# Phi prepared a batch earlier, fixed buffers, and a cast on VectorE in the exponential slots

## The chip, the cores and the metric

The kernel runs on one core of a Trainium2 chip. The metric is the device time of one execution in microseconds (us). The core's engines are TensorE (PE in the profile; PEld is its weight load, which overlaps), VectorE (DVE), ScalarE (ACT), GpSimd (POOL, almost unused here) and SyncE (SP, which issues most DMAs). Each works through its own queue in order and waits on semaphores for the others.

## What is computed

An attention through 32 memory slots per head, followed by a feed-forward network of 2048 hidden units with a SiLU. There are 8 batches, 8 heads, 576 rows and 64 elements per head, all in float32.

```python
a = softmax(phi, over the 576 rows)             # phi: 8 x 8 x 576 x 32
k_m = einsum('bhsm,bhsd->bhmd', a, k)
v_m = einsum('bhsm,bhsd->bhmd', a, v)
scores = softmax(q @ k_m.T / 8)                 # over the 32 memory slots
attn_out = scores @ v_m
x = attn_out reshaped to (4608, 512)
h = x @ w_in
return (h * sigmoid(h)) @ w_out
```

## The kernel before

Float32 accuracy is reached with pairs: a high part, rounded to the matmul's fp32r type, and a low part, the difference. Every product is then three matmuls (high by high, high by low, low by high).

The kernel never forms the attention output. For a batch `b` it multiplies `v_m` into `w_in` (`p_mm`, a *projection*, line 621, in four blocks of 512 hidden units). That gives a weight of 256 memory rows, `pm`, and the first layer is attention weights by `pm`. The attention weights, split in high and low, are in `aparts`.

Batches 2 to 7, on which the change works, are alike. A batch is 16 **slots**: two halves `t` of the rows, eight pairs `j` of hidden blocks. A slot, called here batch:slot (5:4 is slot 4 of batch 5), is:

- `ffn1s` (L807): 12 matmuls 128x288 into the PSUM tile `h`, of which there is one;
- `forms` (L813 on): ScalarE applies Silu to `h` (L818 for the 512 main columns, into the one buffer `gbuf`; L820 for the 64 left-over ones), casts the first three of seven forms to their high part (L822); VectorE makes the other four forms (L823, L826, L827); ScalarE casts these (L828); VectorE subtracts for the two low parts (L829, L830);
- the slot's **events**: steps of preparing the next batch, and of projecting this one;
- `st_step` (L839) of the slot *before*: 21 products into four PSUM banks by a Strassen-like scheme. After slots 7 and 15 `st_out` (L870, L875) empties the banks: two copies on ScalarE, seven adds on VectorE.

TensorE's order is the order of the code, ScalarE's too from batch 1 on. VectorE's is put by the framework's scheduler, which must keep events' VectorE work behind the slot's last subtraction (`behind`, `last_split`) except for `s_all`. SP's order is that of the code in the first stage and the scheduler's behind it.

The events prepare batch `n = b + 1` while batch `b` runs. They are: `phi_max` (L256 to L259) and `phi_fold` (three steps, L284 to L302), the maximum over all rows; `phi_sub` (L310, L313) subtracts it; `phi_exp` (L317) is the exponential on ScalarE, which needs another activation table than Silu, so that a table load stands before it and one before the next Silu; `e_mm` (L333, L343) sums phi by keys and values, in two parts of two chunks each; `e_tr` transposes; `s_all` (L380 to L389) makes the scores; `s_max`, `s_sub`, `s_exp` (L432, again between two table loads), `s_sum`, `s_norm` are the second softmax; `s_back` (L453, L458) turns it back and `s_low` (L463) makes the low part, for the rows of the first half (FIRST) or of the second (SECOND). The projection copies its bank pair `bg` out in `p_split`: the high part on ScalarE (L644), the low part on VectorE (L646). `bg` exists once; `e_mm`, `e_tr` and `s_all` use it too.

In batches 2 to 6 the events stood in these slots: 1 `phi_max` and third projection, 2 `phi_fold`, 3 `phi_sub`, then the fourth projection, 4 `phi_exp`, 5 and 7 `e_mm`, 6 `s_back`'s second half (SECOND), 8 `e_tr`, 9 `s_all`, 10 `s_max` and `s_sub`, 11 `s_exp`, 12 `s_sum`, 13 `s_norm` and first projection, 14 `s_back` and `s_low` (FIRST), 15 second projection. Batch 7 prepares nothing and only projects.

After an odd batch the 64 left-over rows of two batches are worked off (`left_split`, L680 and L682, and `left_st`, the `lsum` tiles of L839).

phi, scores and attention weights shared a pool of two buffers (`att`), and the two halves of q one of two (`q`).

Of the kernel before, what the change touches and what calls it, by code (L numbers as in the profile page):

```python
# [48 lines left out]
def attn_ffn_kernel(  # L49
# [155 lines left out]
    at = [dict() for _ in range(B)]  # L205
# [163 lines left out]

    def s_all(b):  # L370

        sc = at[b]["sc"] = sb.tile([P, 2, S], F32, tag="att", name=f"sc{b}")
        bg, left = bgtile(), beside_h(S - 512)
        kvT = at[b]["kvT"]
        w = 512 - HALF
        for hf, f, n in ((0, 0, HALF), (1, 0, w), (1, w, HALF - w)):
# [9 lines left out]
        for p in range(2):
            nc.vector.transpose(sc[:, p, 512:], left[p])
        for p in range(2):
            nc.vector.transpose(sc[:, p, :512], bg[:, p])  # L389

    def s_mm(b, hf):
        if "sc" not in at[b]:
            at[b]["sc"] = sb.tile([P, 2, S], F32, tag="att", name=f"sc{b}")
        pt = banks(b)
        kvT, q = at[b]["kvT"], at[b]["q", hf]
        for r in range(NR):
            for p in range(2):
# [6 lines left out]
        at[b]["sp", hf] = pt
        if b:
            s_turn(b, hf)
# [39 lines left out]
            at[b][x] = aparts[:, k, b == 1].rearrange("p (g s) -> p g s", g=2)  # L446

    def s_back(b, u):
        at[b]["aT"] = sb.tile([P, 2, S], F32, tag="att", name=f"aT{b}")
        set_parts(b)  # L450
        aT, sc = at[b]["aT"], at[b]["sc"]
        for p in range(2):
            nc.vector.transpose(aT[:, p], sc[:, p])  # L453
        s_high(b, u)
# [13 lines left out]
    first = {}  # L468
    UW = (2 * HM, 2 * HM + P)
# [328 lines left out]
    def ffn1s(b, t, j):  # L798
# [11 lines left out]
                    n += 1  # L810
        return h

    def forms(b, t, j, h):  # L813


        g = form_src
        w = MAIN // 2
        nc.scalar.activation(gbuf[:, :MAIN].rearrange("p (i f) -> p i f", i=2), h[:, :, :w], AF.Silu)  # L818
        o = b % 2 * LEFT + t * (LEFT // 2)
        nc.scalar.activation(gleft[:, 2 * j : 2 * j + 2, o : o + LEFT // 2], h[:, :, w:HALF], AF.Silu)  # L820
        hi, lo = form_high[j % 2], form_low[j % 2]
        nc.scalar.activation(hi[:, :3], g[:, 1:4], AF.Copy)  # L822
# [4 lines left out]
        s4 = nc.vector.tensor_tensor(g[:, 7], g[:, 3], g[:, 6], op=ALU.subtract)  # L827
        nc.scalar.activation(hi[:, 3:], g[:, 4:], AF.Copy)  # L828
# [93 lines left out]
    def ev(b, slot, fn, *a):  # L922
        events.setdefault((b, slot), []).append((fn, a))

    for b in range(B):
        n = b + 1
        if b == 0:
            for j in range(2, DFF // CW):
                ev(b, 2 * j - 1.5, p_mm, b, j * CW, CW)
        elif b == 1:  # L930
            ev(b, 0, win_save)
            for j in range(1, NJ):
                ev(b, 4 * j - 3, p_mm, b, j * JW, JW)
# [25 lines left out]
        ev(b, 3 if b > 1 else sub + 0.5, phi_sub, n)  # L959
        ev(b, ex, phi_exp, n)  # L960
        if n < 3:
            ev(b, em, e_mm, n)
            ev(b, 14 if b == 0 else em + 1, load_kv, n + 1, range(FULLC if b == 0 else 2))
        else:
            ev(b, em, e_mm, n, range(2))
            ev(b, em, load_kv, n, range(2, FULLC))
            ev(b, em + 2, e_mm, n, range(2, FULLC))
            if n + 1 < B:
                ev(b, em + 2, load_kv, n + 1, range(2))
# [7 lines left out]
        if n + 1 < B:  # L977
            ev(b, s1, load_q, n + 1, 0)
# [5 lines left out]
        u = ALL if n < 3 else FIRST  # L984
        ev(b, sk, s_back, n, u)
        ev(b, sk, s_low, n, u)
        if n + 1 < B:
            ev(b, sk, load_phi, n + 1)
# [247 lines left out]
```

## Time and profile before

| | us |
|---|---|
| median of 3 runs | 718.83 (717.64 to 719.99) |
| the profiled execution | 719.41 |
| its span, first to last instruction | 717.6 |

The page's section 2 cuts the span in 40 slices; each digit is an engine's busy share in tenths, PEclk the granted clock:

```profile
PE   8999999999998999989999899989999989999997
DVE  4898799789756568947768567884776848786653
ACT  3878674535335455454625545554452454654440
PEclk9999999999999999999999999999999999999999
```

TensorE is busy nearly everywhere; VectorE and ScalarE have room in the mean. A group such as "PE h L807" is read as engine, written tile and line; "<-ACT phi L317" behind a wait says that ScalarE's instruction of line 317 ended it. Since slots are all alike, a longer slot in the same trace shows what an event costs.

### The profile page before, as it was taken

The page shows a single profiled execution, that of the slowest core. Times are in us where ns is not written, and L with a number is a line of the kernel's source. Part 1 is how long each engine was busy: PE and PEld are TensorE (multiplying, and loading weights), DVE is VectorE, ACT ScalarE, POOL GpSimd, SP SyncE. Part 2 cuts the span into 40 slices and gives each one's busy share as a digit, 9 for nine tenths or more (in the row PEclk, how much of TensorE's full clock was granted, in tenths as well). Part 3 has the DMA queues.
Part 4 walks back from the last instruction along what each step waited for, and adds up shares of the span by engine and source line. Part 5 has one row for each costly group of instructions (what it writes and reads, how often), then busy time and mean ns, then how long its engine had stood idle before and what let it go on. Part 6 is the DMA issues. An engine that isn't in the chain of part 4 may idle for free.

```text
span 717.6 us, 14742 instructions
## 1 busy us (share of the span) xinstructions
PE 684.0 (95%) x5932; PEld 601.9 (84%) x5932; DVE 516.8 (72%) x1109; ACT 367.1 (51%) x674; POOL 0.7 (0%) x6
## 2 busy tenths in 40 slices
PE   8999999999998999989999899989999989999997
PEld 3577777888888889879898888879989889889997
DVE  4898799789756568947768567884776848786653
ACT  3878674535335455454625545554452454654440
POOL 0000000000000000000000000000000000000000
PEclk9999999999999999999999999999999999999999
DMA  9997956304531344025330154303631013210001
GB/s 345 330 357 251 338 215 225 104 30 156 195 102 61 110 178 152 31 73 214 120 122 16 60 192 155 122 1 134 213 111 71 16 61 129 91 76 2 30 1 45
DMA packets 32948, 93.90 MB, mean 131 GB/s; under 512 B 2928, under 2 KB 13296, under 8 KB 29296
## 3 DMA queue, kind: packets, MB, share of 16 engines
q1 hardware_dynamic: 31936, 90.19, 36.1%
q10 hardware_dynamic: 944, 2.77, 1.0%
q8 instruction: 47, 0.77, 0.4%
q14 instruction: 21, 0.17, 0.1%
HBM read 77.22 MB, written 15.73 MB: 130 GB/s over the span
## 4 chain that ended last, share of the span: by engine, by line
PE 52%; DVE 20%; ACT 10%; issue 4%; DVEq 0%; ACTq 0%
PE sum L839 18%; PE h L807 12%; PE acc L706 7%; PE lsum L839 5%; PE h L665 4%; ACT aparts L828 3%; DVE gbuf L823 2%; PE bg L628 2%; DVE pm L646 2%; DVE oo L875 2%; DVE gbuf L826 2%; DVE gbuf L827 2%; PE bg L333 2%; ACT gbuf L818 2%; DVE gparts L830 2%
## 5 line engine op out<-in xcount | busy, mean ns | idle before, releaser
L807 PE MATMUL h<-aparts,pm 128*128 128x288 f32 x1152 | 169.0, 296 | 6.4 <-ACT gleft L820 6.4
L807 PEld LDWEIGHTS h<-aparts,pm 128*128 128x128 f32 x1152 | 157.0, 188 | 7.6 <-ACT gleft L820 7.4
L818 ACT ACTIVATE gbuf<-h 128x512 f32<-128x512 f32 x96 | 57.4, 598 | 129.4 <-PE h L807 129.2
L823 DVE TENSOR_TENSOR gbuf<-gbuf 128x256 f32<-128x256 f32 x96 | 40.5, 422 | 114.4 <-ACT gbuf L818 113.9
L828 ACT ACTIVATE aparts<-gbuf 128x512 fp32r<-128x512 f32 x96 | 60.7, 633 | 100.2 <-DVE gbuf L827 100.2
L839 PE MATMUL sum<-wo_hi,aparts 128*128 128x256 f32 x384 | 106.5, 298 | 0.0
L839 PE MATMUL sum<-kept,aparts 128*128 128x256 f32 x576 | 102.4, 287 | 2.2 <-DVE oo L875 2.2
L839 PE MATMUL sum<-wo_lo,aparts 128*128 128x256 f32 x384 | 101.9, 287 | 0.0
L839 PEld LDWEIGHTS sum<-wo_hi,aparts 128*128 128x128 f32 x384 | 74.7, 195 | 21.4 <-ACT gleft L820 14.2
L839 PEld LDWEIGHTS sum<-kept,aparts 128*128 128x128 f32 x576 | 84.3, 195 | 3.4 <-DVE oo L875 3.4
L706 PE MATMUL acc<-wo_hi,gparts 128*128 128x512 f32 x256 | 86.4, 397 | 0.3 <-DVE gparts L682 0.2
L830 DVE TENSOR_TENSOR gparts<-gbuf,aparts 128x512 fp32r<-128x512 f32 x96 | 66.5, 693 | 20.5 <-ACT aparts L828 20.5
L839 PEld LDWEIGHTS sum<-wo_lo,aparts 128*128 128x128 f32 x384 | 75.0, 195 | 0.0
L839 PE MATMUL sum<-wo_hi,gparts 128*128 128x256 f32 x384 | 72.8, 282 | 0.0
L839 PE MATMUL sum<-kept,gparts 128*128 128x256 f32 x288 | 65.5, 282 | 0.0
L706 PEld LDWEIGHTS acc<-wo_hi,gparts 128*128 128x128 f32 x256 | 47.8, 188 | 14.4 <-DVE t L789 1.7
L839 PEld LDWEIGHTS sum<-wo_hi,gparts 128*128 128x128 f32 x384 | 59.7, 191 | 0.0
L665 PEld LDWEIGHTS h<-aparts,pm 128*128 128x128 f32 x372 | 51.8, 188 | 7.7 <-issue 2.3
L665 PE MATMUL h<-aparts,pm 128*128 128x288 f32 x372 | 56.3, 299 | 1.3 <-DVE aparts L463 1.0
L829 DVE TENSOR_TENSOR gparts<-gbuf,aparts 128x384 fp32r<-128x384 f32 x96 | 52.9, 551 | 0.1
L706 PE MATMUL acc<-wo_lo,gparts 128*128 128x512 f32 x128 | 50.4, 394 | 0.8 <-DVE wo_lo L182 0.7
L822 ACT ACTIVATE aparts<-gbuf 128x384 fp32r<-128x384 f32 x96 | 50.4, 525 | 0.0
(198 smaller groups left out, 977.5 us busy)
## 6 DMA issues: line engine op xcount, KB each, us to landing
win<-win_saved SPq DMA_DIRECT2D x24, 1024.0 KB, 4.8
kv<-in_kv SPq DMA_DIRECT2D x28, 516.0 KB, 4.7
q<-in_q SPq DMA_DIRECT2D x16, 576.0 KB, 6.7
raw<-in_w_in SPq DMA_DIRECT2D x14, 512.0 KB, 7.5
out<-oo SPq DMA_DIRECT2D x27, 256.0 KB, 2.2
raw<-in_w_out SPq DMA_DIRECT2D x6, 1024.0 KB, 5.7
win_saved<-win SPq DMA_DIRECT2D x4, 1024.0 KB, 8.9
phi<-in_phi SPq DMA_DIRECT2D x7, 576.0 KB, 5.3
```

The source lines that it names most:

```text
L333: nc.tensor.matmul(pt[p][M * r : M * (r + 1), :KVW], e[:, p, c, M * r : M * (r + 1)], kvt[c][:, p, r], start=c == 0, stop=False, skip_grou ...
L628: nc.tensor.matmul(bg[M * r : M * (r + 1), p, :w].rearrange("p (k f) -> p k f", f=P), kvT[D * p : D * (p + 1), 1, r], src[D * p : D * (p + ...
L665: nc.tensor.matmul(h[:, hf, :HALF], wt[:, p, fs], a[:, p, hf * HALF : (hf + 1) * HALF], start=n[hf] == 0, stop=n[hf] == 5, skip_group_chec ...
L706: nc.tensor.matmul(acc[key], gt[:, cs], wt[:, fc], start=fc == 0 and n == 0, stop=fc == NFC - 1 and n == 2)
L807: nc.tensor.matmul(h[:, i, :HALF], wt[:, p, f : f + P], a[:, p], start=n == 0, stop=n == 5)
L818: nc.scalar.activation(gbuf[:, :MAIN].rearrange("p (i f) -> p i f", i=2), h[:, :, :w], AF.Silu)
L822: nc.scalar.activation(hi[:, :3], g[:, 1:4], AF.Copy)
L823: nc.vector.tensor_tensor(g[:, 4:6], g[:, :1].broadcast_to([P, 2, P]), g[:, 1:3], op=ALU.subtract)
L828: nc.scalar.activation(hi[:, 3:], g[:, 4:], AF.Copy)
L829: behind(nc.vector.tensor_tensor(lo[:, :3], g[:, 1:4], hi[:, :3], op=ALU.subtract).ins, s4)
L830: last_split.append(nc.vector.tensor_tensor(lo[:, 3:], g[:, 4:], hi[:, 3:], op=ALU.subtract))
L839: nc.tensor.matmul(sums[bank][:, place * Q : (place + 1) * Q], gt[:, k], wt, start=bank not in begun, stop=True, skip_group_check=True,)
```

## The change

Three things are done in batches 2 to 6.

1. *Slots.* From batch 3 on, `phi_max`, `phi_fold` and `phi_sub` for the batch after next are done in slots 7, 11 and 15; in batch 2 they are done for batch 3 in slots 1 to 3, as before, and for batch 4 in slots 12, 13 and 15. `phi_exp`, `e_mm`, `e_tr` and `s_all` move up by two slots from batch 3 on (`phi_exp` in slot 2). `s_max` moves from 10 to 9 there. The fourth projection moves from 3.5 to 2, and SECOND from 6 to 1. Loads move with them: the second half of q to slot 2, phi to the slot of the second `e_mm`, the first half of q to the slot of `s_all`.
2. *Buffers.* phi, scores and attention weights get fixed buffers: `x`, `y`, and from batch 3 on the attention weights stand where the second half of q was (`q1`).
3. *The cast.* In the two slots of a batch with an exponential, the high part of the last four forms is cast by VectorE (L832 after) and both low parts are one subtraction (128x896, L833 after).

The diff, cut:

```diff
     def load_phi(b):
-        t = sb.tile([P, PHW], F32, tag="att", name=f"phi{b}")
+        t = sb.tile([P, PHW], F32, tag="y" if b == 2 else "x", name=f"phi{b}", bufs=1)
...
     def load_q(b, hf, few=False):
-        t = sb.tile([P, NR, HALF], F32, tag="q", name=f"q{b}_{hf}", bufs=2)
+        t = sb.tile([P, NR, HALF], F32, tag=f"q{hf}", name=f"q{b}_{hf}", bufs=1)
...
-        sc = at[b]["sc"] = sb.tile([P, 2, S], F32, tag="att", name=f"sc{b}")
+        sc = at[b]["sc"] = sb.tile([P, 2, S], F32, tag="x" if b == 2 else "y", name=f"sc{b}", bufs=1)
...
     def s_back(b, u):
-        at[b]["aT"] = sb.tile([P, 2, S], F32, tag="att", name=f"aT{b}")
+        tag = ("x", "y")[b - 1] if b < 3 else "q1"
+        at[b]["aT"] = sb.tile([P, 2, S], F32, tag=tag, name=f"aT{b}", bufs=1)
...
+    def exp_slots(b):
+        return () if b == B - 1 else (4, 11) if b == 2 else (2, 11)
...
         s4 = nc.vector.tensor_tensor(g[:, 7], g[:, 3], g[:, 6], op=ALU.subtract)
+        if t * NP + j in exp_slots(b):
+            nc.vector.tensor_copy(hi[:, 3:], g[:, 4:])
+            last_split.append(nc.vector.tensor_tensor(lo, g[:, 1:], hi, op=ALU.subtract))
+            return hi, lo
         nc.scalar.activation(hi[:, 3:], g[:, 4:], AF.Copy)
...
+    def steady(b, n):
+        early = b > 2
+        if not early:
+            ev(b, 1, phi_max, n)
+            for i in range(3):
+                ev(b, 2, phi_fold, n, i)
+            ev(b, 3, phi_sub, n)
+        ex = exp_slots(b)[0]
+        ev(b, 2, load_q, n, 1)
+        ev(b, ex, phi_exp, n)
+        ev(b, ex + 1, e_mm, n, range(2))
+        ev(b, ex + 1, load_kv, n, range(2, FULLC))
+        ev(b, ex + 3, e_mm, n, range(2, FULLC))
+        ev(b, ex + 4, e_tr, n)
+        ev(b, ex + 5, s_all, n)
+        ev(b, 9 if early else 10, s_max, n, ALL)
+        ev(b, 10, s_sub, n, ALL)
+        ev(b, 11, s_exp, n, ALL)
+        ev(b, 12, s_sum, n, ALL)
+        ev(b, 13, s_norm, n, ALL)
+        ev(b, 14, s_back, n, FIRST)
+        ev(b, 14, s_low, n, FIRST)
+        for k in range(3):
+            ev(b, 10 + 2 * k, win_load, n, k)
+        for k in range(2):
+            ev(b, 13 + 2 * k, p_mm, n, k * JW, JW)
+        m = n + 1
+        if m < B:
+            ev(b, ex + 3, load_kv, m, range(2))
+            ev(b, ex + 3, load_phi, m)
+            ev(b, ex + 5, load_q, m, 0)
+            ev(b, 7 if early else 12, phi_max, m)
+            for i in range(3):
+                ev(b, 11 if early else 13, phi_fold, m, i)
+            ev(b, 15, phi_sub, m)
...
             ev(b, 1, p_mm, b, 2 * JW, JW)
-            ev(b, 3.5, p_mm, b, 3 * JW, JW)
             if b > 2:
-                ev(b, 6, s_high, b, SECOND)
-                ev(b, 6, s_low, b, SECOND)
-        if n == B:
+                ev(b, 1, s_high, b, SECOND)
+                ev(b, 1, s_low, b, SECOND)
+            ev(b, 2, p_mm, b, 3 * JW, JW)
+            if n < B:
+                steady(b, n)
             continue
```

How instructions stand in the queues follows, at three places. Names are the program's, with its numbers. Lines behind 810 of the old code have other numbers in the new: L818, L820, L822 and L828 become L821, L823, L825 and L835; L823, L826, L827, L829 and L830 become L826, L829, L830, L836 and L837; L436 to L446 keep theirs; L453 and L463 become L454 and L464.

*ScalarE at phi's exponential in batch 5*, before, slot 4:

```order
L818 ACTIVATE gbuf_82<-h_5148 128x512
L820 ACTIVATE gleft_80<-h_5148 128x2x32
L822 ACTIVATE aparts_81<-gbuf_82 128x384
L828 ACTIVATE aparts_81<-gbuf_82 128x512
L317 ACT_TABLE_LOAD
L317 ACTIVATE phi6_4825<-phi6_4825 128x1152
L818 ACT_TABLE_LOAD
```

and after, slot 2:

```order
L821 ACTIVATE gbuf_82<-h_5046 128x512
L823 ACTIVATE gleft_80<-h_5046 128x2x32
L825 ACTIVATE aparts_81<-gbuf_82 128x384
L644 ACTIVATE pm_5076<-bg_5067 128x1024
L317 ACT_TABLE_LOAD
L317 ACTIVATE phi6_4348<-phi6_4348 128x1152
L821 ACT_TABLE_LOAD
```

The cast of the last four forms is gone from ScalarE's queue; the copy of the fourth projection (`pm` from `bg`), which stood a slot ahead, is now in front of the exponential.

*VectorE from the end of slot 15 of batch 4 into batch 5*, before (L823 is the first operation of 5:0):

```order
L829 TENSOR_TENSOR gparts_79<-gbuf_82,aparts_81 128x384
L830 TENSOR_TENSOR gparts_79<-gbuf_82,aparts_81 128x512
L646 TENSOR_TENSOR pm_4881<-bg_4872,pm_4881 128x1024
L823 TENSOR_TENSOR gbuf_82<-gbuf_82 128x256
L826 TENSOR_TENSOR gbuf_82<-gbuf_82 128x128
```

and after (L826 is the first operation of 5:0):

```order
L837 TENSOR_TENSOR gparts_79<-gbuf_82,aparts_81 128x512
L310 TENSOR_TENSOR phi6_4348<-phi6_4348,am_4688 128x512
L646 TENSOR_TENSOR pm_4899<-bg_4890,pm_4899 128x1024
L313 TENSOR_TENSOR phi6_4348<-phi6_4348,am_4688 64x128
L310 TENSOR_TENSOR phi6_4348<-phi6_4348,am_4688 128x512
L313 TENSOR_TENSOR phi6_4348<-phi6_4348,am_4688 64x128
L826 TENSOR_TENSOR gbuf_82<-gbuf_82 128x256
```

The four operations of `phi_sub` for batch 6 have come in around L646, ahead of the forms of the next batch's first slot. After batches 3 and 5 they likewise stand ahead of the left-over casts, the first of which stood ahead of L646 before.

*VectorE in batch 2, slot 13's end to slot 15's beginning*, before (L453 and L463 are `s_back` and `s_low`):

```order
L442 TENSOR_TENSOR sc3_2583<-sc3_2583,ssm_2754 128x1152
L646 TENSOR_TENSOR pm_2813<-bg_2804,pm_2813 128x1024
L823 TENSOR_TENSOR gbuf_82<-gbuf_82 128x256
L826 TENSOR_TENSOR gbuf_82<-gbuf_82 128x128
L827 TENSOR_TENSOR gbuf_82<-gbuf_82 128x128
L829 TENSOR_TENSOR gparts_79<-gbuf_82,aparts_81 128x384
L830 TENSOR_TENSOR gparts_79<-gbuf_82,aparts_81 128x512
L453 STREAM_TRANSPOSE aT3_2859<-sc3_2583 128x576 x2
L463 TENSOR_TENSOR aparts_81<-aT3_2859,aparts_81 128x2x288
```

and after, from L826 of slot 14 on:

```order
L826 TENSOR_TENSOR gbuf_82<-gbuf_82 128x256
L286 TENSOR_REDUCE qm_2824<-mxt_2822 128x8
L829 TENSOR_TENSOR gbuf_82<-gbuf_82 128x128
L292 COPY qz_2826<-qm_2824 32x8 x4
L830 TENSOR_TENSOR gbuf_82<-gbuf_82 128x128
L294 TENSOR_REDUCE fm_2831<-qz_2826 32x8
L836 TENSOR_TENSOR gparts_79<-gbuf_82,aparts_81 128x384
L296 COPY fm_2831<-fm_2831 32x8 x3
L837 TENSOR_TENSOR gparts_79<-gbuf_82,aparts_81 128x512
L301 COPY wide_2837<-fm_2831 128x256
L454 STREAM_TRANSPOSE aT3_2883<-sc3_2584 128x576
L302 STREAM_TRANSPOSE am_2836<-wide_2837 128x256
```

The steps of the fold for batch 4 stand between the forms' operations and inside `s_back`'s pair of transposes; `phi_max` for batch 4 stands the same way in slots 12 and 13. From batch 3 on the whole fold stands in slot 11, behind the slot's last subtraction.

More of the change, by code (lines that the diff above doesn't have):

```diff
@@ L392, in s_mm @@
         if "sc" not in at[b]:
-            at[b]["sc"] = sb.tile([P, 2, S], F32, tag="att", name=f"sc{b}")
+            at[b]["sc"] = sb.tile([P, 2, S], F32, tag="x" if b == 2 else "y", name=f"sc{b}", bufs=1)
         pt = banks(b)
@@ L533, in f_part @@
         if key not in first:
-            tag = {"sc": "att", "mx": "smx", "sm": "ssm"}[key]
-            bufs = 2 if tag == "att" else 1
-            first[key] = sb.tile([P, sum(UW) // (S * 2 // width)], F32, tag=tag, name=f"f{key}", bufs=bufs)
+            tag = {"sc": "y", "mx": "smx", "sm": "ssm"}[key]
+            first[key] = sb.tile([P, sum(UW) // (S * 2 // width)], F32, tag=tag, name=f"f{key}", bufs=1)
         n = width * UW[0] // (2 * S)
@@ L947, in attn_ffn_kernel @@
             (4, 5, 6, 7.5, 9, 9.5, 11.5, 12.5, 13, 13.5, 13.5, 14) if b == 0
-            else (1, 2, 3, 5, 9, 10, 10, 11, 12, 13, 13, 14) if b == 1
-            else (1, 2, 4, 5, 8, 9, 9, 10, 11, 12, 13, 14)
+            else (1, 2, 3, 5, 9, 10, 10, 11, 12, 13, 13, 14)
         )
@@ L958, in attn_ffn_kernel @@
                 ev(b, sub, phi_fold, n, i)
-        ev(b, 3 if b > 1 else sub + 0.5, phi_sub, n)
+        ev(b, sub + 0.5, phi_sub, n)
         ev(b, ex, phi_exp, n)
[L961 to L969, printed above, removed]
+        ev(b, em, e_mm, n)
+        ev(b, 14 if b == 0 else em + 1, load_kv, n + 1, range(FULLC if b == 0 else 2))
         ev(b, tr, e_tr, n)
@@ L976, in attn_ffn_kernel @@
             ev(b, s0, s_all, n)
-        if n + 1 < B:
-            ev(b, s1, load_q, n + 1, 0)
+        ev(b, s1, load_q, n + 1, 0)
         ev(b, sx, s_max, n, ALL)
@@ L983, in attn_ffn_kernel @@
         ev(b, sn, s_norm, n, ALL)
[L984 to L988, printed above, removed]
+        ev(b, sk, s_back, n, ALL)
+        ev(b, sk, s_low, n, ALL)
+        ev(b, sk, load_phi, n + 1)
         if b == 0:
@@ L992, in attn_ffn_kernel @@
             for k in range(3):
-                ev(b, 6 + k if b == 1 and k < 2 else 10 + 2 * k, win_load, n, k)
+                ev(b, 12 if k == 2 else 6 + k, win_load, n, k)
             for k in range(2):
-                ev(b, (12 if b == 1 else 13) + 2 * k, p_mm, n, k * JW, JW)
+                ev(b, 12 + 2 * k, p_mm, n, k * JW, JW)
     slots = [1.5, 1.5] + [2 * j - 1 if k == "i" else min(2 * j - 0.5, 12.5) for k, i in later for j in [i - 1 if k == "i" else i]]
```

## The prediction

> A slot is written batch:slot, and "+x" counts from its first L807 matmul. Durations are microseconds of the one profiled execution.
>
> **What bounds the kernel now.** The page comes first: busy time by engine.
>
> ```profile
> PE 684.0 (95%) x5932; PEld 601.9 (84%) x5932; DVE 516.8 (72%) x1109; ACT 367.1 (51%) x674; POOL 0.7 (0%) x6
> ```
>
> TensorE is the bound, so only its stalls can be won. The view of waits (engine, line, waited for: total, times, longest) names them:
>
> ```profile
> PE bg L333 <- ACT phi L317: 12.2, 5, 3.2
> PE h L807 <- ACT gleft L820: 6.4, 5, 1.3
> ```
>
> Five waits of the key/value sums (`e_mm`, L333) for phi's exponential and five of L807 for ScalarE: one of each in batches 2 to 6. What a wait really costs stands in the view of windows, cut at slot borders (start:end, length, busy time of PE, PEld, DVE, ACT, POOL, granted clock, DMA share, GB/s): slot 5 of batches 2 to 6, then 7:5, 5:12, 4:9 and 7:9.
>
> ```profile
> 223.35:232.21 8.86, 6.89 (x68) 6.45 (x67) 3.83 (x9) 6.14 (x8) 0.00 (x0) 0.81 0.37 117
> 304.25:314.27 10.02, 6.86 (x68) 6.30 (x66) 4.99 (x11) 6.14 (x8) 0.00 (x0) 0.83 0.31 103
> 398.27:407.16 8.89, 6.92 (x67) 6.30 (x66) 3.82 (x9) 6.14 (x8) 0.00 (x0) 0.81 0.34 114
> 478.96:489.05 10.09, 6.93 (x68) 6.31 (x66) 4.99 (x11) 6.15 (x8) 0.00 (x0) 0.83 0.30 104
> 573.07:580.40 7.33, 5.36 (x67) 4.92 (x66) 3.14 (x8) 6.12 (x8) 0.00 (x0) 1.00 0.25 70
> 652.18:656.27 4.09, 4.09 (x35) 4.09 (x34) 2.17 (x5) 1.77 (x5) 0.00 (x0) 1.00 0.00 0
> 517.57:523.12 5.55, 4.27 (x35) 4.07 (x33) 1.59 (x5) 5.12 (x7) 0.00 (x0) 1.00 0.32 136
> 421.27:427.49 6.22, 5.91 (x83) 4.85 (x82) 5.35 (x16) 2.93 (x7) 0.00 (x0) 1.00 0.51 180
> 668.59:673.62 5.03, 4.36 (x35) 4.15 (x34) 4.69 (x12) 2.63 (x7) 0.00 (x0) 1.00 0.25 93
> ```
>
> A bare slot is 4.09. In 6:5 TensorE idles 7.33 - 5.36 = 1.97, in 5:5 10.09 - 6.93 = 3.16. The timeline shows the chain in 5:4 that makes such a wait (start, length, engine, line, and in brackets the idle time before and what ended it):
>
> ```profile
> 480.72 0.63 ACT L828 ACTIVATE aparts<-gbuf 128x512 fp32r<-128x512 f32 x1 [2.74 <-DVE gbuf L827]
> 481.37 1.28 ACT L317 ACT_TABLE_LOAD   x1
> 482.66 1.16 ACT L317 ACTIVATE phi<-phi 128x1152 f32<-128x1152 f32 x1
> ```
>
> ScalarE stood 2.74 for VectorE before the cast L828, and only then came the table, 1.29 later the exponential, and behind it a table for Silu again. 6:5 without its wait would be 5.36. 4:5 idles the same 1.97 (8.89 - 6.92), but its clock was granted at 0.81 and it took 1.56 more. Of five such waits four lost clock; slot 12 (stall 5.55 - 4.09 = 1.46) lost none.
>
> **The change: what it wins.** The undisturbed chain of 7:8, its products in 7:9, and a projection (`p_mm`) in 5:15:
>
> ```profile
> 664.48 1.76 PE L807 MATMUL h<-aparts,pm 128*128 128x288 f32 x12
> 666.28 0.60 ACT L818 ACTIVATE gbuf<-h 128x512 f32<-128x512 f32 x1 [1.73 <-PE h L807]
> 666.77 0.22 ACT L820 ACTIVATE gleft<-h 128x64 f32<-128x64 f32 x1
> 666.91 0.53 ACT L822 ACTIVATE aparts<-gbuf 128x384 fp32r<-128x384 f32 x1
> 672.21 0.75 PE L839 MATMUL sum<-kept,aparts 128*128 128x256 f32 x4 [0.67 <-DVE oo L875]
> ...
> 532.64 1.76 PE L807 MATMUL h<-aparts,pm 128*128 128x288 f32 x12
> 534.33 1.09 PE L628 MATMUL bg<-win,kvT 64*32 64x512 f32 x16
> ...
> L644 ACT ACTIVATE pm<-bg 128x1024 fp32r<-128x1024 f32 x28 | 28.3, 1012 | 1.5 <-PE bg L628 1.5
> ```
>
> In an exponential slot ScalarE is free after its first cast, at 667.44 - 664.48 = +2.96. In slot 2 of batches 3 to 6 the copy L644 goes first: +3.97; table +5.27, exponential +6.45. Slot 2 lasts 5.28 (it holds a projection), so `e_mm` comes at 5.28 + 1.69 = +6.97: margin 0.5. In batch 2 (slot 4, no projection) the exponential ends at +5.44 and `e_mm` comes at 4.1 + 1.7 = +5.8. So the wait goes: 45.19 (the five slots) - 5 x 5.36 = **18.4**. In slot 11 the score exponential ends at +5.44, the table at +6.73, the left-over Silu (0.71 after Silu's start, as in 7:8) at +7.44; L807 of slot 13 needs it at +8.2. So **5 x 1.46 = 7.3** goes too. Together 25.7.
>
> The VectorE cast itself:
>
> ```profile
> L680 DVE CAST gparts<-gbuf 128x512 fp32r<-128x512 f32 x32 | 13.3, 417 | 12.5 <-ACT gbuf L690 12.5
> L789 DVE TENSOR_TENSOR kept<-wf,kept 128x768 fp32r<-128x768 f32 x3 | 2.9, 951 | 0.0
> L646 DVE TENSOR_TENSOR pm<-bg,pm 128x1024 fp32r<-128x1024 f32 x28 | 34.1, 1219 | 1.3 <-ACT pm L644 1.1
> ```
>
> 0.42 for the cast; the joined subtraction 128x896 does not occur: between 0.95 and 1.22, taken midway at 1.09, against about 1.24 for the two it replaces. At either end the parts are ready about when they were, so I take nothing.
>
> Edits costed at nothing: fixed buffers issue no instruction. SP's moved loads keep cover: q's second half waits for `s_low` of slot 1 and is read in slot 7, over 20 later; kv 2 and 3 leave after `e_mm` in slot 3 and are read 8.2 later (slot 3 and 4, and 1.7 into 5, less 2.8; before: 9.9), the fourth weight block has about 14 and phi over 10. The median landings on the page are 6.7, 4.7, 4.8 and 5.3. SP issues in order, so a late `s_low` would hold kv too; 8.2 against 4.7 is the cover.
>
> **What it costs.** (1) *Slot 9, batches 3 to 6.* `st_out`'s last add gates four products: 0.67 in 7:9, a slot of 5.03. Before, `s_all` stood ahead of them in slot 9 and left a wait of 0.31. Moved to slot 7 it costs 6.22 - 0.31 - 4.09 = 1.82 there, and slot 9 becomes 5.03: 10.94 against 6.22 + 4.09, **0.63 x 4 = 2.5**. Bounds 0 and 0.94 each.
>
> (2) *Slot 15's `phi_sub`.* Four operations; here they are first and last, then batch 4 to 5 and the left-over products after batch 5:
>
> ```profile
> 301.94 0.69 DVE L310 TENSOR_TENSOR phi<-phi,am 128x512 f32<-128x512 f32 x1
> 303.44 0.29 DVE L313 TENSOR_TENSOR phi<-phi,am 64x128 f32<-64x128 f32 x1
> ...
> 463.55 0.41 DVE L875 TENSOR_TENSOR oo<-x,sum 128x256 f32<-128x256 f32 x1
> 464.16 0.64 PE L839 MATMUL sum<-kept,aparts 128*128 128x256 f32 x4
> ...
> 539.14 0.42 DVE L680 CAST aparts<-gleft 128x512 fp32r<-128x512 f32 x1
> 541.34 0.30 PEld L839 LDWEIGHTS lsum<-wo_hi,aparts 128*128 128x128 f32 x2 [0.31 <-DVE aparts L682]
> ```
>
> They take 1.8. From 4 to 5 the last add ended 0.2 ahead of the products, so 1.6 of lateness (0.2 was idle) stalls **1.4**. After batches 3 and 5 the first left-over cast stood ahead of L646 and now stands behind `phi_sub` and L646; the subtraction that gates the third product starts 1.8 + 0.33 later: **2 x 2.15 = 4.3** (bounds 0 and 3.3, with L646 whole). These waits are as long as those that lost clock four times in five: 2 x 1.56 x 0.8 = **2.5**.
>
> The Trainium skill ("TensorE: Matmul & The Clock Gate", Part 1) has the clock halved after an idle window of about 3.4 us. By that these 2.5 would not arise; the 0.81 behind 1.97 disagrees.
>
> (3) *The bank pair `bg`.* The last projection moves from slot 3 to slot 2. In 5:1, as in 7:1, `st_out` runs late; its copy was:
>
> ```profile
> 465.52 1.01 ACT L644 ACTIVATE pm<-bg 128x1024 fp32r<-128x1024 f32 x1
> ```
>
> That is +5.3, and with L646 (1.22) behind it `bg` comes free at +7.6; the projection of slot 2 wants it at +6.97. 0.65 in batch 7, 0.8 in batch 5 (later by its 1.6, less the 1.4 that TensorE waits anyway), **1.4**. Bounds 0 and 1.2 each (L646 whole).
>
> (4) *Batch 2 to 3.* Only here `phi_max` and the fold crowd into slots 12 to 14, with the score steps. Before:
>
> ```profile
> 276.06 1.76 PE L807 MATMUL h<-aparts,pm 128*128 128x288 f32 x12
> 278.81 0.69 ACT L458 ACTIVATE aparts<-aT 128x576 fp32r<-128x576 f32 x1 [2.11 <-DVE aT L453]
> 279.40 0.58 ACT L818 ACTIVATE gbuf<-h 128x512 f32<-128x512 f32 x1
> ...
> 384.29 0.69 DVE L256 TENSOR_TENSOR mt<-phi 128x512 f32<-128x512 f32 x1
> 386.47 0.58 DVE L259 TENSOR_TENSOR mx<-mx,phi 64x128 f32<-64x128 f32 x2
> 214.65 0.44 DVE L284 STREAM_TRANSPOSE mxt<-mx 128x256 f32<-128x256 f32 x1
> 217.61 0.44 DVE L302 STREAM_TRANSPOSE am<-wide 128x256 f32<-128x256 f32 x1
> ```
>
> Silu of slot 15 stands behind L458, which waits for VectorE: +3.34. `phi_max` is 1.65 without the L646 inside it; the fold, 3.4 with a form operation inside, is 3.1: 4.75. Set one behind the other in the new order, from slot 12 on, these leave Silu at +6.9 (1.2 fell into idle time) and L807 of 3:0, due at +5.33, at +7.7: 2.4. Then the forms, `phi_sub` and the adds run on late, and the products of 3:1 wait 2.9 more; a loss of clock would hide in these, since VectorE sets the pace. **5.3.** Bounds: 0, and (8.09 + 0.71 - 5.33) + 2.9 = 6.4.
>
> For batches 3 to 5 I put nothing here: the fold (3.1) is all in slot 11, behind which VectorE reaches slot 13 about 1.0 late, as it does now.
>
> **Sum.** 25.7 - (2.5 + 1.4 + 4.3 + 2.5 + 1.4 + 5.3) = 25.7 - 17.4 = 8.3 won. The profiled execution took 719.41 (span 717.6 and 1.8 around it): 711.1. The median of the runs, 718.83, lies 0.6 below it: **710.5**.
>
> **Rivals.** *Cheap ends:* the clock holds, as in 6:5, and 2 to 3 pays only its second part: 25.7 - 12.5 = 13.2, **706**. For it: one wait in five kept the clock; against: four. The skill's clock rule would give 708 by itself; the rows bear it out once in five.
>
> *The wait stays:* the exponential in slot 2 has 0.5 of margin, behind L644. If it ended 1.5 later, five `e_mm` would wait 1.0: 3.3 won, **715.5**. For it: the thin margin; against: rows 481.37 and 482.66, table and exponential with nothing between. The skill ("ScalarE: Activation LUTs", What ACT_TABLE_LOAD costs) adds a drain of 1.38 us to each switch, which would do just this; those two rows show 1.29 from load to exponential.
>
> *Slower: VectorE's backlog in slots 11 to 15 at every border.* If the fold's 3.1 is not absorbed by slot 13, the last Silu of batches 3, 4 and 5 and all behind it come 3.1 later, and 4 to 5 loses clock as well: 9.3 + 1.6 over my costs, **722** (711.1 + 10.9). It turns slower where over 2.2 of the 3.1 survives each time (3 x 2.2 + 1.6 is the 8.2 won). For it: batch 2 does it; against: slots 12 and 14 have no projection and VectorE is busy 2.2 of a bare 4.09.
>
> **How the numbers follow.** Forecast 0.55, cheap ends 0.20, wait stays 0.12, backlog 0.07, mixtures between 715 and 721 0.06. Under 0.3% (2.2 us, about what a measurement of this kernel can tell from none) counts as the same. Faster: 0.55 + 0.20 + 0.10; slower 0.07; the rest the same. The range leaves out the best of the cheap ends and all above 717: **704 to 717**.
>
> **What would show it.** Right: no row of L333 waiting for L317; slots 5, 3 and 12 at 5.7, 5.3 and 4.1 with clock 1.00; 7:9's wait for the adds in slot 9 of batches 3 to 6; L807 of 3:0 over 2 late behind ScalarE; the left-over products 2 late. Wrong: `e_mm` still waiting, waits at DMA queues, or Silu of slot 15 past +6 in batches 3 to 5.

## The result, and the profile after

| | us |
|---|---|
| before, median of 4 runs beside it | 719.04 |
| after, median of 4 runs | 709.71 (709.62 to 710.63) |
| ratio | 0.9875, 95% interval 0.9856 to 0.9893 |
| profiled execution after | 710.63, span 708.8 |

The change gains 1.25%. One execution of all those shown in this document was slow, 1308.1 of the kernel with the cast alone; its time below, 695.27, is the median of its other three (695.04 to 696.31), where all four give 695.79.

The profile page after, busy time by engine:

```profile
PE 681.1 (96%) x5932; PEld 599.3 (85%) x5932; DVE 521.9 (74%) x1109; ACT 361.1 (51%) x664; POOL 0.7 (0%) x6
```

ScalarE has ten instructions less, the casts, and 6.0 less busy time; VectorE has as many instructions as before and is 5.1 busier. The view of waits after (engine, line, waited for: total, times, longest):

```profile
PE sum L846 <- DVE oo L882: 6.4, 8, 1.5
PE lsum L846 <- DVE aparts L680: 4.1, 2, 2.1
PE h L807 <- ACT gleft L823: 2.2, 1, 2.2
...
PE bg L628 <- DVE pm L646: 1.1, 2, 0.7
...
PE sum L846 <- ACT oo L877: 0.7, 1, 0.7
```

Both old rows, `e_mm` behind the exponential and L807 behind ScalarE five times, are gone. What TensorE waits for now in these batches is VectorE, and at two places (2:15 and 3:1) ScalarE, which is itself held by VectorE. None of these waits ends at a DMA: the moved loads cost nothing, as forecast.

The windows after, cut at the same kind of borders (start:end, length, then busy time of PE, PEld, DVE, ACT, POOL, granted clock, DMA share, GB/s). In order: the `e_mm` slots 2:5 and 4:3; 5:12; `s_all` in 4:7 and the slot of `st_out`'s adds, 4:9; the borders with left-over rows, 3:15 and 5:15; the border from batch 2 to 3, slots 2:15 and 3:1; 5:1; and the projections in 5:2 and 7:2.

```profile
223.36:228.66 5.30, 5.30 (x67) 4.94 (x66) 2.92 (x7) 3.75 (x6) 0.00 (x0) 1.00 0.34 81
...
388.27:393.57 5.30, 5.30 (x67) 4.94 (x66) 3.05 (x6) 4.15 (x6) 0.00 (x0) 1.00 0.35 92
...
509.24:513.35 4.11, 4.11 (x35) 4.11 (x34) 3.78 (x13) 3.74 (x6) 0.00 (x0) 1.00 0.42 175
...
407.67:413.34 5.67, 5.67 (x84) 4.80 (x82) 3.96 (x11) 2.06 (x5) 0.00 (x0) 1.00 0.31 106
417.52:422.55 5.03, 4.36 (x35) 4.14 (x34) 4.68 (x12) 2.64 (x7) 0.00 (x0) 1.00 0.39 129
352.46:373.25 20.79, 18.59 (x145) 16.93 (x143) 14.66 (x31) 4.99 (x9) 0.00 (x0) 0.92 0.21 77
522.75:543.69 20.94, 18.51 (x144) 16.95 (x143) 14.66 (x31) 4.99 (x9) 0.00 (x0) 0.92 0.21 76
271.19:278.86 7.67, 5.49 (x52) 4.28 (x50) 6.76 (x21) 1.97 (x5) 0.00 (x0) 1.00 0.40 137
283.06:291.16 8.10, 5.90 (x51) 4.43 (x50) 7.49 (x21) 3.88 (x8) 0.00 (x0) 1.00 0.17 61
453.68:460.70 7.02, 5.77 (x51) 4.39 (x50) 6.45 (x17) 3.08 (x7) 0.00 (x0) 1.00 0.18 67
460.70:466.75 6.05, 5.36 (x52) 4.29 (x50) 5.29 (x10) 5.24 (x9) 0.00 (x0) 1.00 0.33 100
629.41:635.21 5.80, 5.37 (x52) 4.30 (x50) 5.06 (x9) 4.13 (x7) 0.00 (x0) 1.00 0.01 3
```

An `e_mm` slot that took 7.33 to 10.09 takes 5.30, TensorE busy all through. In the later rows, length less PE busy is TensorE's idle time: 2.2 and 2.4 at the borders with left-over rows (where the clock is at 0.92 besides), 2.2 each in 2:15 and 3:1, 1.25 in 5:1.

The timeline of ScalarE after, in 4:2, shows the chain that once made `e_mm` wait (start, length, engine, line, idle time before in brackets):

```profile
384.75 0.60 ACT L821 ACTIVATE gbuf<-h 128x512 f32<-128x512 f32 x1 [1.42 <-PE h L807]
...
385.84 1.03 ACT L644 ACTIVATE pm<-bg 128x1024 fp32r<-128x1024 f32 x1
386.89 1.28 ACT L317 ACT_TABLE_LOAD   x1
388.18 1.17 ACT L317 ACTIVATE phi<-phi 128x1152 f32<-128x1152 f32 x1
```

The exponential ends at 389.35; `e_mm` follows the twelve matmuls of 4:3, which start at 388.27, at 389.94.

### The profile page after: what moved, and what is told of

Read it like the earlier page. It is cut to its first block, busy times and chain, and to the rows that moved or that the text cites. A ratio compares the mean times of both kernels' runs of the same rounds, so it can differ in the third digit from the quotient of the medians.

```text
span 708.8 us, 14734 instructions
## 1 busy us (share of the span) xinstructions
PE 681.1 (96%) x5932; PEld 599.3 (85%) x5932; DVE 521.9 (74%) x1109; ACT 361.1 (51%) x664; POOL 0.7 (0%) x6
## 4 chain that ended last, share of the span: by engine, by line
PE 61%; DVE 17%; issue 4%; ACT 4%; DVEq 0%; ACTq 0%
PE sum L846 23%; PE h L807 16%; PE acc L706 7%; PE lsum L846 5%; PE h L665 4%; PE bg L628 2%; DVE oo L882 2%; ACT aparts L835 2%; DVE pm L646 2%; DVE gbuf L826 2%; PE accleft L706 2%; PE bg L333 1%; DVE gbuf L829 1%; DVE gbuf L830 1%; DVE aT L454 1%
## 5 line engine op out<-in xcount | busy, mean ns | idle before, releaser
L807 PE MATMUL h<-aparts,pm 128*128 128x288 f32 x1152 | 169.0, 296 | 2.2 <-ACT gleft L823 2.2
L807 PEld LDWEIGHTS h<-aparts,pm 128*128 128x128 f32 x1152 | 157.1, 188 | 3.4 <-ACT gleft L823 2.5
L821 ACT ACTIVATE gbuf<-h 128x512 f32<-128x512 f32 x96 | 57.3, 597 | 140.7 <-PE h L807 140.4
L826 DVE TENSOR_TENSOR gbuf<-gbuf 128x256 f32<-128x256 f32 x96 | 40.4, 421 | 102.8 <-ACT gbuf L821 102.6
L846 PE MATMUL sum<-kept,aparts 128*128 128x256 f32 x576 | 100.8, 284 | 6.4 <-DVE oo L882 6.4
L846 PE MATMUL sum<-wo_hi,aparts 128*128 128x256 f32 x384 | 104.5, 294 | 0.7 <-ACT oo L877 0.7
L846 PE MATMUL sum<-wo_lo,aparts 128*128 128x256 f32 x384 | 100.0, 282 | 0.0
L835 ACT ACTIVATE aparts<-gbuf 128x512 fp32r<-128x512 f32 x86 | 54.4, 633 | 82.7 <-DVE gbuf L830 82.7
L846 PEld LDWEIGHTS sum<-wo_hi,aparts 128*128 128x128 f32 x384 | 72.7, 189 | 22.5 <-ACT gleft L823 10.9
L846 PEld LDWEIGHTS sum<-kept,aparts 128*128 128x128 f32 x576 | 82.5, 191 | 8.0 <-DVE oo L882 8.0
L846 PEld LDWEIGHTS sum<-wo_lo,aparts 128*128 128x128 f32 x384 | 73.1, 190 | 0.0
L837 DVE TENSOR_TENSOR gparts<-gbuf,aparts 128x512 fp32r<-128x512 f32 x86 | 59.4, 691 | 18.0 <-ACT aparts L835 18.0
L825 ACT ACTIVATE aparts<-gbuf 128x384 fp32r<-128x384 f32 x96 | 50.4, 525 | 0.0
L846 PEld LDWEIGHTS sum<-kept,gparts 128*128 128x128 f32 x288 | 47.9, 190 | 0.0
```

The costliest lines, as they stand in the source:

```text
L807: nc.tensor.matmul(h[:, i, :HALF], wt[:, p, f : f + P], a[:, p], start=n == 0, stop=n == 5)
L826: nc.vector.tensor_tensor(g[:, 4:6], g[:, :1].broadcast_to([P, 2, P]), g[:, 1:3], op=ALU.subtract)
L846: nc.tensor.matmul(sums[bank][:, place * Q : (place + 1) * Q], gt[:, k], wt, start=bank not in begun, stop=True, skip_group_check=True,)
```

## Experiments

Seven kernels were run, four in the first group, then two, then one. The ratios are against the kernel before beside them (719.31 in the first group, 718.15 in the others).

| kernel | median us | ratio, 95% interval | span |
|---|---|---|---|
| before, with the cast alone | 695.27 | 0.967 (0.9654 to 0.9686) | 693.4 |
| after, without the cast | 717.35 | 0.9978 (0.9962 to 0.9994) | 714.1 |
| after, `phi_sub` in slot 1 | 703.03 | 0.9779 (0.9763 to 0.9795) | 701.1 |
| after, matmuls to keep the clock | 708.18 | 0.9848 (0.9833 to 0.9862) | 706.4 |
| after, phi not early | 697.04 | 0.9706 (0.969 to 0.9721) | 695.0 |
| after, fold of batch 2 in slot 11 | 709.83 | 0.9873 (0.9852 to 0.9895) | 708.9 |
| after, both `phi_sub` and fold moved | 701.59 | 0.9761 (0.9743 to 0.9779) | 699.6 |

### The cast alone in the kernel before

The theory was that the cast is enough by itself to take the waits away; the rival, that it needs the move. Into the kernel before, with all its slots and buffers, only this goes:

```diff
+        if t * NP + j in (() if b == B - 1 else (4, 11)):
+            nc.vector.tensor_copy(hi[:, 3:], g[:, 4:])
+            last_split.append(nc.vector.tensor_tensor(lo, g[:, 1:], hi, op=ALU.subtract))
+            return hi, lo
         nc.scalar.activation(hi[:, 3:], g[:, 4:], AF.Copy)
```

> The kernel before with nothing but the VectorE cast (and the joined subtraction) in slots 4 and 11 of batches 2 to 6; phi's slots, buffers and projections as before. Theory A (the won time comes from the cast alone: it frees ScalarE at +2.96 of the slot instead of behind the late L827, and the earlier phi only costs): the exponential of slot 4 ends at +5.4, e_mm wants it at +5.8, phi_sub is done by then; all five waits of L333 and all five of slot 12 go, 18.5 + 7.2, and none of the 17 that the change cost at the borders arises: 719.0 - 25.7 = 693.3, between 692 and 697. Rival B (phi has to be earlier for the cast to help, because phi_sub in slot 3 is what makes the exponential late): half or less of it, 706 to 712.

It won 24.0, over two and a half times what the whole change wins, and it is the fastest kernel here. Its windows of slot 4:5 (`e_mm`) and of 3:15 (left-over rows):

```profile
388.04:393.34 5.30, 5.30 (x68) 4.94 (x66) 2.96 (x8) 3.75 (x6) 0.00 (x0) 1.00 0.35 92
347.63:364.82 17.19, 17.01 (x145) 15.60 (x144) 12.50 (x26) 4.96 (x9) 0.00 (x0) 1.00 0.35 128
```

`e_mm` no longer waits, although it stands in slot 5 with the exponential in slot 4, and the border has kept its 17.19. The timeline of ScalarE in slot 5:4 says why:

```profile
462.31 0.53 ACT L822 ACTIVATE aparts<-gbuf 128x384 fp32r<-128x384 f32 x1
462.85 1.28 ACT L317 ACT_TABLE_LOAD   x1
464.14 1.17 ACT L317 ACTIVATE phi<-phi 128x1152 f32<-128x1152 f32 x1
```

In the kernel before, 2.74 of waiting and 0.63 of casting stood between the first cast and the table. Here the table comes at once. It is less the cast's 0.63 that is won than the place in ScalarE's queue where it waited for VectorE.

### The move alone

The changed kernel with the four lines of the cast taken out again, all else as it is:

```diff
-        if t * NP + j in exp_slots(b):
-            nc.vector.tensor_copy(hi[:, 3:], g[:, 4:])
-            last_split.append(nc.vector.tensor_tensor(lo, g[:, 1:], hi, op=ALU.subtract))
-            return hi, lo
```

> The changed kernel without the VectorE cast: ScalarE casts in all slots; slots and buffers as in the change. Theory A: ScalarE reaches L644 1.2 later in slot 2, so e_mm of batches 3 to 6 waits about 0.7 each, batch 2's about 2.5 with clock lost (1.6), slot 11 delays L807 of slot 13 by 0.5 in batches 3 to 6 and 1.4 in batch 2: 3 + 4 + 2 + 1.4, 10 slower than the changed kernel, 720, so that moving phi alone gives nothing (717 to 723). Rival B (the earlier phi carries the gain): 709 to 713.

The move and the buffers alone give 0.2%. The windows of slot 2:5 and of the border 3:15:

```profile
223.46:230.90 7.44, 5.35 (x67) 4.92 (x66) 3.23 (x8) 6.11 (x8) 0.00 (x0) 1.00 0.24 58
357.24:376.58 19.34, 16.96 (x144) 15.59 (x143) 14.29 (x30) 4.98 (x9) 0.00 (x0) 1.00 0.22 83
```

2:5, which isn't moved, waits its 2.09. In batches 3 to 6 `e_mm` still waits, but only 0.35 to 0.57, and slot 12 is 4.6 instead of 5.55. So the move does shorten the waits (the `e_mm` slots and slots 12 by 18.0 together), and gives most of it back: 11.1 at the borders and 3.4 in slots 2 and 7 to 9. In this execution the borders were 2.1 longer than before, with the clock at 1.00; in the profile of the full change they were 3.6 and 3.7 longer, at 0.92.

### `phi_sub` out of slot 15

The costliest suspect: `phi_sub` in slot 1 of the batch that uses its phi, right ahead of the exponential of slot 2.

```diff
-            ev(b, 15, phi_sub, m)
...
                 ev(b, 1, s_low, b, SECOND)
+            if 2 < b < B - 1:
+                ev(b, 1, phi_sub, n)
             ev(b, 2, p_mm, b, 3 * JW, JW)
```

> The changed kernel with phi_sub of batches 4 to 7 in slot 1 of the batch that uses it instead of slot 15 of the batch ahead. Theory A (phi_sub in slot 15 makes the left-over casts, the adds of st_out and so the products late): slot 15 of batches 3 and 5 falls back from 20.8 and 20.9 to 17.2 (7.3), 5:1 from 7.0 to 5.3 (1.7), 3:1 from 8.1 to about 6.5 (1.6): 10.6 faster than the changed kernel, about 699 (697 to 702). Rival (these waits come of the moved loads or of SECOND in slot 1 and stay, or phi_sub in slot 1 makes the exponential of slot 2 late): within 3 of 709.7.

6.7 of the 10.6 that were expected were won, and the time is above the expected range. The slots that it aimed at are 9.8 shorter in its profile (3:15 and 5:15 by 6.8, 5:1 and 3:1 by 1.5 each), but 2.2 come back in slots 2 and 3. Rows of its waits, and its windows of 3:15 and 3:3, show what came new:

```profile
PE bg L628 <- DVE pm L646: 1.6, 3, 0.9
PE bg L333 <- DVE pm L646: 1.4, 4, 0.5
```

```profile
351.52:369.00 17.48, 17.23 (x144) 15.63 (x143) 12.80 (x27) 4.99 (x9) 0.00 (x0) 1.00 0.25 92
...
294.98:300.82 5.84, 5.36 (x67) 4.96 (x66) 4.25 (x7) 4.15 (x6) 0.00 (x0) 1.00 0.34 96
```

The borders with left-over rows are back at 17.48 (17.20 before), so `phi_sub` in slot 15 was nearly their whole cost, clock and all. But the four operations now push L646, and the bank pair `bg` comes free later for the projection of slot 2 and for `e_mm` of slot 3. 2:15 stays at 7.68, and 3:1 only comes down from 8.10 to 6.61.

### Matmuls that keep TensorE busy at the left-over border

Seven matmuls on data that nobody reads, ahead of the left-over products after batches 3 and 5; nothing of the result depends on them.

```diff
+                if n == 0 and 1 < b < B - 1:
+                    keep_warm(ps.tile([P, 2, 512], F32, tag="h", name="warm", bufs=1)[:, 0], 7)
```

> The changed kernel with seven dummy matmuls 128x512 (bf16, into the free h banks) on TensorE between the last products of batches 3 and 5 and the left-over products, where TensorE stands 2.05 now. They compute nothing that is used. Theory A (the wait of 2.05 costs a second time, by the lowered clock behind it, as the prediction had it): slot 15 of batches 3 and 5 falls from 20.8 and 20.9 to about 19.4, 2 x 1.5 = 3.0 faster, 706.7, with the granted clock 1.00 behind the wait. Rival (the 20.8 is only late work on VectorE; the clock falls but hides nothing): no change, 709.7.

The windows of slot 3:0, then of 3:1, then of 3:15:

```profile
278.81:284.51 5.70, 5.70 (x33) 5.70 (x34) 5.36 (x12) 2.98 (x6) 0.00 (x0) 0.70 0.00 0
284.51:291.12 6.61, 5.54 (x51) 4.33 (x50) 6.05 (x17) 3.88 (x8) 0.00 (x0) 1.00 0.20 74
352.40:372.04 19.64, 18.74 (x152) 16.24 (x151) 14.67 (x31) 4.99 (x9) 0.00 (x0) 1.00 0.22 82
```

By the medians it won 1.5, half of the 3.0 expected; the span of the profiled execution is 2.4 shorter. The border went from 20.79 to 19.64 with the clock at 1.00, though the wait for VectorE is the same 2.2 (1.68 of matmuls and 0.53 of idle time before the first product). The 1.15 and 1.31 that the two borders won are clock alone. Without a wait that lowers the clock these borders take 19.34, as in the run without the cast, so the clock's price is 20.79 - 19.34 = 1.45 and 1.6. The two rows on top show a loss that costs nothing: behind the 2.2 of waiting in 2:15 the clock fell this time, 3:0 took 5.70 instead of 4.20, and 3:1 took 6.61 instead of 8.10. The sums are 12.31 and 12.30.

### Everything but the early phi

Buffers, cast, fourth projection in slot 2 and SECOND in slot 1 stay; phi goes back to where it was.

```diff
-        return () if b == B - 1 else (4, 11) if b == 2 else (2, 11)
+        return () if b == B - 1 else (4, 11)
...
-        early = b > 2
+        early = False
...
-            ev(b, 7 if early else 12, phi_max, m)
-            for i in range(3):
-                ev(b, 11 if early else 13, phi_fold, m, i)
-            ev(b, 15, phi_sub, m)
```

> The changed kernel with the cast, the buffers and the fourth projection and SECOND in slots 2 and 1, but phi prepared where it was (phi_max, fold and phi_sub for the next batch in slots 1 to 3, exponential in slot 4, scores in slot 9). Theory A, all that separates 709.7 from the 695.8 of the cast alone is the earlier phi (slot 15, the crowd of batch 2, s_all ahead of slot 9), but for the bank pair of the projection in slot 2: slots 3:15 and 5:15 back at 17.2, 2:15 and 3:0 and 3:1 bare of the 5.3, waits of L628 for L646 in 3:2, 5:2 and 7:2 of 0.2 to 0.9 each: 697.5 (696 to 699). Rival B, the buffers or the earlier projection and SECOND carry part of it: over 701, with new waits in slots 1 and 2 or at loads.

697.04, as the first theory had it. From its waits:

```profile
PE bg L628 <- DVE pm L646: 2.5, 3, 0.9
PE sum L846 <- DVE oo L882: 2.2, 6, 0.7
```

Buffers, projection and SECOND carry the 2.5 of three waits for `bg` (3:2, 5:2, 7:2) and little else; nearly all that parts 709.7 from 695.3 is phi, prepared a batch earlier.

### The crowd in slots 12 to 14 of batch 2

`phi_max` for batch 4 into slot 9 and its fold into slot 11 of batch 2, in the changed kernel:

```diff
-            ev(b, 7 if early else 12, phi_max, m)
+            ev(b, 7 if early else 9, phi_max, m)
             for i in range(3):
-                ev(b, 11 if early else 13, phi_fold, m, i)
+                ev(b, 11, phi_fold, m, i)
```

> The changed kernel, but in batch 2 phi_max for batch 4 stands in slot 9 and its fold in slot 11, not in 12 and 13. Theory A, the 5.3 from batch 2 to 3 come from these steps crowding with the score steps in slots 12 to 14: L807 of 3:0 waits under 1 for ScalarE instead of 2.2 and the border costs 3 or less: 707.3 (706.5 to 708.3). Rival B, the backlog is phi_sub and the second projection in slot 15 alone: 2:15 stays at 7.7 and the time within 0.7 of 709.7.

The step that was blamed was right, the expected time was not: no gain, 709.83. The windows of 2:15 and 3:1:

```profile
272.08:277.41 5.33, 5.33 (x52) 4.33 (x50) 4.28 (x9) 2.23 (x5) 0.00 (x0) 1.00 0.44 148
...
281.50:290.22 8.72, 6.88 (x52) 5.39 (x50) 7.85 (x20) 4.06 (x8) 0.00 (x0) 0.87 0.18 63
```

2:15 lost its wait (7.67 to 5.33), so the crowd makes it. But 2:12 became 0.6 longer, and in 3:1 `st_out`'s adds still came late, with VectorE busy 7.85 of 8.72, and the clock fell: PE was busy 6.88 for work that took 5.90 in the profile of the change, and the slot behind it took 5.85 instead of 5.31. In this execution lateness went and 1.5 of clock took its place. The four executions order by their granted clock: 710.83 and 710.34 at 0.992, 709.33 at 0.994 and 708.20, in the range that was expected, at 0.997. Rival B's account (the backlog is that of slot 15 alone) fits the time and not 2:15.

### Both of them

> The changed kernel with both edits: phi_sub in slot 1 of the batch that uses it, and in batch 2 phi_max for batch 4 in slot 9 and its fold in slot 11. Theory A, the border from batch 2 to 3 has two causes that add up: the crowd in slots 12 to 14 makes L807 of 3:0 wait (2.3), and phi_sub ahead of the adds of st_out makes the products of 3:1 wait (the 1.8 left of it with the crowd gone); with both gone 2:15 is 5.3 and 3:1 at most 5.6, no clock is lost there, 2:12 stays 0.6 longer: 703.0 less 2.3, less 1.0, plus 0.6 is 700.3 (699.3 to 701.5). Rival B, VectorE's sum of work before 3:2 decides and the wait only moves on: 3:1 over 6.3 or 3:2 over 6.3, and a time of 702 or more.

The edits of the third and the sixth kernel together took 701.59, 1.4 less than `phi_sub` in slot 1 alone: just above the range of the first theory, and below the rival's. From its waits:

```profile
PE sum L846 <- DVE oo L882: 4.3, 7, 0.7
PE bg L628 <- DVE pm L646: 2.4, 3, 1.0
PE bg L333 <- DVE pm L646: 1.4, 4, 0.5
```

2:15 is 5.32 (2.36 won), 2:12 is 0.6 longer, and 3:1 went only from 6.61 to 6.23 while 3:2 went from 5.56 to 6.32, waiting 0.95 for `bg`. Both theories hold in part: there are two causes, but of the 2.36 won on the first 0.9 comes back as other waits that VectorE makes.

## Why the prediction came out

Forecast 710.5, measured 709.71. The waits that went and the places that pay for it are those that it named, each about as large as it said, with two things that it did not see. That the costs agree to 0.1 is partly luck: terms that are off by up to 0.6 cancel.

**What the change wins.** The five `e_mm` slots went from 45.19 to 5 x 5.30, 18.7 (18.4 forecast), and the five slots 12 are 7.1 shorter (7.3). The margin of the chain in slot 2 is 389.94 - 389.35 = 0.6 (0.5 forecast). That rules out the rival in which the wait stays. The Trainium skill's drain of 1.38 us at each table switch ("ScalarE: Activation LUTs", What ACT_TABLE_LOAD costs) would have used up that margin; rows 386.89 and 388.18 again show 1.29 from load to exponential. The joined subtraction, taken midway between two rows at 1.09, is 1.09 in the groups by line:

```profile
L833 DVE TENSOR_TENSOR gparts<-gbuf,aparts 128x896 fp32r<-128x896 f32 x10 | 10.9, 1092 | 1.3
```

**What it costs**, term by term, from slot lengths before and after:

| step | forecast | measured |
|---|---|---|
| (1) slot 9, batches 3 to 6 | 2.5 | 1.9 |
| (2) batch 4 to 5 | 1.4 | 1.7 |
| (2) left-over borders, wait and clock | 4.3 + 2.5 | 7.3 |
| (3) bank pair `bg` | 1.4 | 1.3 |
| (4) batch 2 to 3 | 5.3 | 5.3 |
| sum | 17.4 | 17.5 |

In (1) `s_all` costs 5.67 - 4.09 = 1.58 in its new slot and not 1.82: TensorE's part of it was put too high (of the 5.91 busy in 4:9 before, 0.27 belongs to the slot of the adds, which has 4.36 without `s_all`). Slots 7 to 9 of batch 4 are 5.67, 4.19 and 5.03, against two bare slots of 4.10 and the 6.22 of 4:9 for the same work. In (2) the wait was right (19.34 - 17.20 = 2.14, twice 4.3), and the clock fell both times, 3.0 instead of 2.5 that a chance of 0.8 had given. All four executions of the change have a granted clock of 0.994 or 0.995, about what two falls make (last section). The order of the operations was as forecast; the timeline of VectorE at 3:15, first and last of `phi_sub`, L646 and the first left-over cast, and the product that waits for it:

```profile
359.24 0.68 DVE L310 TENSOR_TENSOR phi<-phi,am 128x512 f32<-128x512 f32 x1
359.84 1.22 DVE L646 TENSOR_TENSOR pm<-bg,pm 128x1024 fp32r<-128x1024 f32 x1
...
361.87 0.29 DVE L313 TENSOR_TENSOR phi<-phi,am 64x128 f32<-64x128 f32 x1
362.18 0.43 DVE L680 CAST aparts<-gleft 128x512 fp32r<-128x512 f32 x1
```

```profile
362.76 0.48 PE L846 MATMUL lsum<-wo_hi,aparts 128*128 128x256 f32 x1 [2.05 <-DVE aparts L680]
```

Only here does the wait end earlier in the chain than was said: the first product waits for the cast, 2.05, and the third for the subtraction but 0.15. In (4) the two parts are 2.35 (forecast 2.4) and 2.9, and that a loss of clock hides there was seen in the run with the extra matmuls. It doesn't hide in 3:1 itself, as the run with the fold in slot 11 shows. So neither half of the cheap ends came: the clock fell, and 2 to 3 paid both parts. For the borders of batches 3 to 5 the forecast put nothing on slots 12 to 14, and they are 4.11, 5.30 and 4.10: the rival of a backlog at every border did not come.

25.8 - 17.5 = 8.3, as forecast. The span fell by 8.8; 0.4 of the rest is slot 13, 0.1 shorter in each of batches 3 to 6.

**What it did not see.** First, the 25.7 were worked out for move and cast together, and never for each alone. The cast by itself takes 18.1 off the `e_mm` slots and 6.7 off slots 12; the move by itself 14.2 and 3.8. The two are remedies for the same waits: the second adds 1.0 to the first, and the 17.5 of cost come with the move. From 695.3 to 709.7 the runs in between give the steps: buffers, fourth projection and SECOND 1.8; phi early as such 4.6 (697.04 to 701.59: `st_out`'s adds uncovered in slot 9, waits for `bg`, 2:12 and 3:1); the crowd of batch 2 another 1.4; `phi_sub` in slot 15 another 6.7. These are differences of medians from different groups, each median sure to about 1.3 (0.0018 of 718, half an interval). The two small steps rest on the profiled spans, which differ by 1.6 and 1.5 (693.4 to 695.0, 699.6 to 701.1); the order of the large ones is not in doubt. They also hold for this order only: the crowd's 1.4 was measured with `phi_sub` moved, and with it in place moving the crowd gave nothing.

Second, whether a wait loses clock is not a matter of chance within an execution: it depends on where the wait lies on a grid of 3.41 us (last section). The prediction took it as a chance of four in five, counted over the waits of one execution.

The clock rule of the Trainium skill ("TensorE: Matmul & The Clock Gate", Part 1), an idle window of about 3.4 us before the clock is halved, was set aside in the prediction because a wait of 1.97 had lost clock. The runs bear that out at 2.05, and in 3:1 of the run with the fold in slot 11 at 0.56 and 1.25 within one slot. The length of the window agrees with the traces, where each fall in these batches lasts 3.41 at a granted 0.50; it need not be idle throughout.

**Left open.** Where the grid lies when an execution starts: the first full clock came 3.99 to 6.86 into the span in the nine profiled executions. No kernel left the cast on ScalarE and put it behind the exponential, so that the place in the queue, and not VectorE's doing the work, wins the time is read from the timeline and not tested by itself. Nor was a version tried that removes the remaining waits of the fastest kernel (0.3 a batch in slot 9).

## What to carry to other kernels

When an instruction of one engine waits in a queue ahead of what another engine needs, look first for a way to take the waiting instruction out of that queue; moving the whole chain to an earlier time costs room elsewhere, here on VectorE at every batch border. Where a change holds two remedies for one wait, price each alone before adding their common costs. Work put into the last slot before a border delays everything that the border needs in order, and when it is moved on it meets the next user of the same engine.

## What the hardware showed unexpectedly

The same wait costs clock in one execution and none in the next. The 2.09 in 2:5 without the cast left the clock at 1.00, where 1.97 in the same slot of the kernel before had left it at 0.81; the 2.05 at 3:15 lost 1.45 in the profile of the change and nothing without the cast; the 2.2 in 2:15 lost nothing in the profile of the change, and 1.5 in the run with the extra matmuls, which come long after it. What is lost is nearly always the same, 1.45 to 1.6, whether the longest wait ahead was 1.25 (that 3:1) or 3.16 (5:5 before).

The granted clock shows what decides, as far as these traces go. Each fall in these batches lasts 3.41 at 0.50, and falls begin only at the borders of a grid of 3.41: in the kernel before at 228.07, 309.99, 402.15 and 484.07, which are 24, 27 and 24 such steps apart. The windows cut on this grid around the wait of 2:15, two of the change and then two of the run with the extra matmuls (length less PE busy is idle time, the third number from the end the granted clock):

```profile
274.09:277.50 3.41, 2.59 (x21) 2.38 (x20) 3.31 (x9) 0.34 (x1) 0.00 (x0) 1.00 0.78 288
277.50:280.92 3.42, 2.06 (x16) 2.06 (x17) 2.38 (x6) 2.63 (x6) 0.00 (x0) 1.00 0.00 0
...
276.51:279.93 3.42, 1.25 (x10) 1.12 (x9) 2.60 (x7) 1.73 (x4) 0.00 (x0) 1.00 0.16 65
279.93:283.34 3.41, 3.41 (x18) 3.41 (x17) 3.18 (x7) 2.58 (x5) 0.00 (x0) 0.50 0.00 0
```

In the change the grid splits the wait into 0.82 and 1.36, and the clock holds; in the other run 2.17 lie in one stretch, and the next stretch runs at 0.50. From batch 2 on, up to the last 4 us, the nine profiled executions have nine stretches with 1.97 or more of idle time, and each was followed by a fall. Between that and 1.46 there are two: 1.50 (3:1 with the fold in slot 11) was followed by one, 1.73 (2:15 with `phi_sub` in slot 1) was not. No stretch with 1.46 or less was.

So the same kernel can lose more or less from one execution to the next. The ten executions without the cast, with five waits of 1.5 to 2.2 in these batches, fall into groups by their granted clock: four at 0.998 or more took 715.85 to 716.03, two at 0.996 took 717.20 and 717.49, four at 0.988 to 0.992 took 718.56 to 720.34. The kernel with both edits, which has no wait over 1.0 in these batches, took 701.43 to 701.74.
